# Memory rows of a recurrent attention block: transposed by VectorE out of PSUM ahead of the sum, with the output's sum moved behind the next q projection

## The chip, the cores and the metric

The kernel runs on one core of a Trainium2 chip. The metric is device time in microseconds (us); three runs of the kernel before gave 1015.4, 1016.96 and 1017.25, median 1016.96. The engines are named as in the profile: PE is TensorE (PEld its weight loads), DVE is VectorE, ACT is ScalarE, POOL is GpSimd, SP is the engine that issues most DMAs.

## What is computed

A transformer block over one sequence of 2048 rows of 640 numbers. The attention is recurrent: the sequence is cut into 64 segments of 32 rows, and each segment is attended together with 8 memory rows, which are the first 8 output rows of the segment before. So segment s+1 cannot be projected in full before the output projection of segment s has given its memory rows. A feed-forward network (640 to 1728 to 640, squared ReLU) follows.

```python
mem = mem0
for s in range(n_seg):                       # 64 segments of 32 rows
    xs = x[:, s * seg_len:(s + 1) * seg_len, :]      # x is layer-normed
    h = jnp.concatenate([mem, xs], axis=1)           # 8 + 32 rows
    q, k, v = (jnp.einsum('btd,dhe->bhte', h, W) for W in (Wq, Wk, Wv))   # 32 heads of 128
    p = _softmax(jnp.where(mask, jnp.einsum('bhqe,bhke->bhqk', q, k) * scale, -1e9))
    o = jnp.einsum('bhte,hed->btd', jnp.einsum('bhqk,bhke->bhqe', p, v), Wo)
    mem = o[:, :M, :]
    outs.append(o[:, M:, :])
h = x + jnp.concatenate(outs, axis=1)
h2 = h + ffn(_layernorm(h))
```

## The kernel before, in words

**Start.** SP issues the loads of wv, wq and wk (`load_w`, L117: five DMAs of 128 partitions and 1 MB each per weight, chunk c holding rows 128c to 128c+127 of the weight) and then wo in six DMAs (`load_wo`). `start` projects the first rows while these come in; step 0's output projection needs wo.

**A step** (`step`, L379) is one segment. The 8 memory rows and the first 24 rows of the segment are 32 "main" rows; the last 8 rows of each segment ("tails") are projected four segments at a time and ahead of need, in small units that serve as filling work. The main rows stand transposed in `hT4` (128 partitions x 5 chunks x 4 segments x 32 rows), so that a projection (`proj`, L196) is twenty matmuls with 32 columns of `hT4` as weights and 512 columns of wq, wk or wv streaming, five chunks for each of four column groups of PE. In order PE does: q half 0, k half 0, q half 1, k half 1 (L206), the memory rows' scores (`scores`, L417, which needs q spread by POOL into `qz` and k half 0 flipped), a part of v, the tokens' scores (L488), the rest of v between softmax parts, attention values (L448, L453), then the output projection `wo_rounds` (L238) into `pw`. Each projection is copied out of PSUM by ACT into `row` (L222, L224, L404 for the last one in halves) and flipped in 32x32 blocks by DVE into qT or kT (L227, L407).

**From output to memory rows.** `wo_rounds` puts four partial results into `pw`: partitions 64*kh + 32*ch + row, where kh is one of two halves of the heads that must be summed and ch one of two halves of the 640 columns. `wo_out` (L241) copies the upper 64 partitions by ACT (`otmp`, L245, 64x320 f32) and adds on DVE (`o`, L246). The columns in each half are interleaved by 64 (`wov2`, L229), so that `mem_to_hT` (L312) can turn the 8 memory rows with twenty small matmuls against an identity (`pm`, L316) and one DVE copy (L318) into the next segment's columns of `hT4`. `store_main` (L339) sends the other 24 rows to DRAM (`o_all`).

**Order.** Each engine runs its instructions in the order in which the program issues them; nothing reorders them. Filling work sits in lists: `fill` (tail projections L206 and the tails' output projection L238 on `oTt`), `late` (DVE flips and LayerNorm statistics, run at the start of the next step), `mid` and `win`. Ahead of `mem_to_hT` a step runs four or six fill units, and the rest behind it. `token_out` (ACT, two copies, L364) stands behind `wo_out`. `tk`, `otmp` and other short-lived tiles share one buffer; `sm`, `pm` and `pw` share one PSUM bank (pool `chn`).

**Afterwards** the FFN runs in four blocks of 512 rows; `prep_sum` (L631) adds the attention's rows to x.

Of the kernel before, what the change touches and what calls it, by code (L numbers as in the profile page):

```python
# [9 lines left out]
ALU = mybir.AluOpType  # L10
AX = mybir.AxisListType
F32 = mybir.dt.float32
BF16 = mybir.dt.bfloat16
# [3 lines left out]
def kernel(  # L17
# [16 lines left out]
    nc = tc.nc  # L34
    _, S, D = A_x.shape
    _, H, E = A_Wq.shape
    M = A_mem0.shape[1]
    SEG = 32
    G = 4
    HG = H // G  # L40
    HE = H * E
    EG = HE // G
    DC = D // 128
    DH = D // 2
    NB = S // 128
    NS = S // SEG
    HD = 24
# [13 lines left out]
    const = ctx.enter_context(tc.tile_pool(name="const", bufs=1))  # L61
    mm = ctx.enter_context(tc.tile_pool(name="mm", bufs=3, space=bass.MemoryType.PSUM))
    chn = ctx.enter_context(tc.tile_pool(name="chn", bufs=1, space=bass.MemoryType.PSUM))
# [4 lines left out]
    s1 = ctx.enter_context(tc.tile_pool(name="s1", bufs=1))  # L68
    s2 = ctx.enter_context(tc.tile_pool(name="s2", bufs=2))

    o_all = dram.tile([S, D], BF16)
# [4 lines left out]
    wo = wts.tile([128, H, D], BF16)  # L76

    ident = const.tile([128, 128], BF16)
    o_ring = [const.tile([128, DH], BF16, name="o%d" % k) for k in range(5)]
    o0 = o_ring[-1]  # L80
    nc.vector.memset(o0[0:64], 0.0)
    make_identity(nc, ident[:])
    mhalf = const.tile([128, 1], F32)
    nc.vector.memset(mhalf[:], -0.5)
# [11 lines left out]
    for g in range(G):  # L96
        r = slice(32 * g, 32 * g + 32)
# [6 lines left out]
    nc.vector.memset(oT[:], 0.0)  # L104
    oTts = [const.tile([128, H, 32], BF16, name="oTt%d" % k) for k in range(2)]

    for o in o_ring:
        nc.gpsimd.memset(o[64:128], 0.0)

    ctx.enter_context(tc.manual_schedule(engines=None))  # L110

    def head(p):
# [3 lines left out]

    def load_w(w, src):  # L117
        w2d = src.rearrange("d h e -> d (h e)")
        for c in range(DC):
            nc.sync.dma_start(out=w[:, c * HE:(c + 1) * HE], in_=w2d[c * 128:(c + 1) * 128, :])  # L120

    xts = {}

# [9 lines left out]
        xts["t", g] = xt  # L133

    load_x(0)
    for ch in range(2):
        nc.scalar.dma_start(out=o0[32 * ch:32 * ch + M, :].rearrange("m (c f) -> m c f", f=64),
                            in_=A_mem0[0].rearrange("m (c t f) -> t m c f", t=2, f=64)[ch])
    load_tail_rows(0)
    load_w(wv, A_Wv)  # L140

# [19 lines left out]
    hT4s, hTts, tails = {}, {}, {}  # L161
# [5 lines left out]
    def ln_norm(b):  # L167
        mv, rs = xns[b]
        xn = s1.tile([128, D], BF16, tag="xn", name="xn")
        xt = xts.pop(b)  # L170
        nc.vector.tensor_scalar(out=xn[:], in0=xt[:], scalar1=mv[:, 0:1], scalar2=rs[:, 0:1],
                                op0=ALU.subtract, op1=ALU.mult)
        xns[b] = xn

    def ln_transpose(b):
# [50 lines left out]
    def flip(row, dst, n):  # L226
        nc.vector.transpose(out=dst[:, n * 16:(n + 1) * 16, 0:32], in_=row.rearrange("p (h e) -> p h e", e=32))  # L227

    wov2 = wo[:].rearrange("p h (c t f) -> p h t c f", t=2, f=64)  # L229

    def wo_rounds(lhs, pw, h0, h1):

        for h in range(h0, h1):
            for kh in range(2):
                for ch in range(2):
                    j = kh * 2 + ch
                    p = h // 8 * 16 + kh * 8 + h % 8
                    nc.tensor.matmul(pw[32 * j:32 * j + 32, 0:DH], lhsT=lhs(p), rhs=wov2[:, head(p), ch],  # L238
                                     start=(h == 0), stop=(h == 15))

    def wo_out(pw):  # L241
        o = o_ring[0]
        o_ring.append(o_ring.pop(0))
        tmp = s1.tile([128, DH], F32, tag="tk", name="otmp")
        nc.scalar.copy(out=tmp[0:64], in_=pw[64:128, 0:DH])  # L245
        nc.vector.tensor_tensor(out=o[0:64], in0=pw[0:64, 0:DH], in1=tmp[0:64], op=ALU.add)  # L246
        return o

    fill, late, mid, win = [], [], [], []

    def run(q, n):
        while n > 0 and q:
            q.pop(0)()
            n -= 1
# [38 lines left out]
    def wo_tail_units(b):  # L293
        st = {}

        def out():
            o = wo_out(st["ps"])
            dst = o_all[:].rearrange("(b s t) d -> b s t d", s=4, t=SEG)
            for ch in range(2):
                nc.sync.dma_start(out=dst[b, :, HD:SEG, ch * DH:(ch + 1) * DH], in_=o[32 * ch:32 * ch + 32, :])  # L300

        def unit(k):
            def f():
                if k == 0:
                    st["ps"] = mmtile()
                wo_rounds(lambda p: oTts[b % 2][:, p, :], st["ps"], k * 16 // 10, (k + 1) * 16 // 10)
                if k == 9:
                    late.append(out)
            return f
        return [unit(k) for k in range(10)]  # L310

    def mem_to_hT(o, hT4, sp):  # L312
        pm = chn.tile([128, 512], F32, tag="ch", name="pm")
        for c in range(DC):
            for q in range(4):
                nc.tensor.matmul(pm[32 * q:32 * q + 32, c * M:(c + 1) * M], lhsT=o[:, (2 * c + q % 2) * 32:(2 * c + q % 2 + 1) * 32],  # L316
                                 rhs=ident[:, q // 2 * 32:q // 2 * 32 + M], start=True, stop=True)
        nc.vector.tensor_copy(out=hT4[:, :, sp, 0:M], in_=pm[:, 0:DC * M].rearrange("p (c m) -> p c m", m=M))  # L318

    def tails_in(b, sp, which="qk", h0=0, h1=H):  # L320
        q, k = [tails[b][w][:].rearrange("p h (k s) -> p h s k", s=4)[:, h0:h1, sp, :] if w in which else None for w in "qk"]
# [5 lines left out]
    vt4s, stores = {}, []  # L327
    vt_d = dram.tile([NB, 4, 128, 2 * E], BF16)

# [8 lines left out]

    def store_main(o, s):  # L339
        for ch in range(2):  # L340
            nc.sync.dma_start(out=o_all[s * SEG:s * SEG + HD, ch * DH:(ch + 1) * DH],
                              in_=o[32 * ch + M:32 * ch + 32, :])

    oTg = oT[:].rearrange("p (n g j) q -> p n g j q", n=2, g=G)
    back = []
# [33 lines left out]
    def step(b, sp, v=None):  # L379
        s = b * 4 + sp  # L380
        last = s == NS - 1
        hT4 = hT4s[b]
# [4 lines left out]
        run(late, 3)  # L387
        if sp == 1 and b + 1 < NB:
            tails_v_in(b + 1, nc.sync)

        def project(which, w, dst, n, between=None):
            if ready:
                if between:
                    between()
                return
            ps = mmtile()
            proj(w, "columns", lhs, n, ps, 0, DC)
            row = rowtile()
            if not between:
                evac_row(which, row[:], ps[:])  # L400
                flip(row[:], dst, n)
                return
            for u in range(2):
                nc.scalar.copy(out=row[:, u * 256:(u + 1) * 256], in_=ps[:, u * 256:(u + 1) * 256])  # L404
            between()
            for u in range(2):
                nc.vector.transpose(out=dst[:, n * 16 + u * 8:n * 16 + u * 8 + 8, 0:32],  # L407
                                    in_=row[:, u * 256:(u + 1) * 256].rearrange("p (h e) -> p h e", e=32))
# [49 lines left out]
            evac(n == 0, oTg[:, n, :, :, 0:M], po[:, :, c0:c0 + 4 * M].rearrange("p g (j m) -> p g j m", m=M))  # L458

        project("q", wq, qT, 0)  # L460
        if not last and not ready:
            spread(0)
        if not last:
# [55 lines left out]
        tk = s1.tile([128, HG, NK], F32, tag="tk", name="tk")  # L519
# [5 lines left out]
        pw = chn.tile([128, 512], F32, tag="ch", name="pw")  # L525
# [4 lines left out]
        if not last:  # L530
# [14 lines left out]
                                op=ALU.mult)  # L545
        pk = s1.tile([128, HG, 32], BF16, tag="pk", name="pk")
        nc.gpsimd.tensor_tensor(out=pk[:], in0=ek[:, :, 0:SEG], in1=rk[:].unsqueeze(2).to_broadcast([128, HG, SEG]),
                                op=ALU.mult)

        o = wo_out(pw)  # L550
        if s:
            token_out(s - 1, po)
        if s > 1:
            store_main(o, s - 2)
        outs = [win.pop(0)()] if win else []
        for f in outs:
            f()
        if not last:
            run(fill, 4 if outs else 6)
            mem_to_hT(o, hT4s[(s + 1) // 4], (s + 1) % 4)  # L560
            tails_in((s + 1) // 4, (s + 1) % 4)
        run(mid, 2)
        run(fill, 100)
# [3 lines left out]
        for u in range(2):  # L567
            nc.gpsimd.tensor_tensor(out=pTx[:, u], in0=pTt[:, u, HD:32].unsqueeze(1).to_broadcast([128, 4, TL]),
                                    in1=same[:], op=ALU.mult)
# [60 lines left out]

    def prep_sum(t, k, got):  # L631
        ot, fx = got
        fv = fx.rearrange("p (c t f) -> p t c f", t=2, f=64)
        nc.vector.tensor_tensor(out=fv, in0=ot.rearrange("p (t c f) -> p t c f", t=2, f=64), in1=fv, op=ALU.add)
        return fx

    def prep_norm(t, k, ht, mv, rs):
# [81 lines left out]
    load_w(wq, A_Wq)  # L719
    ln_stats(("t", 0))  # L720
    ln_transpose(0)()
    mem_to_hT(o0, hT4s[0], 0)
    ln_norm(("t", 0))
    load_w(wk, A_Wk)
    load_wo()
# [2 lines left out]
    v0 = start()  # L728
    halves = [h for b in range(8, NB) for h in (tail_units(b, "v")[:DC], tail_units(b, "v")[DC:])]
    for b in range(NB):  # L730
        for sp in range(4):
            run(soon, 1)
            if sp == 0 and b + 2 < NB:
                load_x(b + 2)
# [5 lines left out]
            if b == 0 and sp == 2:  # L740
                fill += tail_units(7, "v")[DC:]
            if 0 < b < NB - 1 and 0 < sp < 3:
                fill += tail_units(b + 1, "vqk"[sp])
# [28 lines left out]
            e = b * 4 + sp - (NS - 7)  # L772
# [30 lines left out]
    for t in range(S // NT):  # L803
# [6 lines left out]
        for fc in range(FC):  # L810
            ps = mmtile()
            for c in range(DC):
                if fc < FFULL:
                    nc.tensor.matmul(ps[:], lhsT=w1[:, c, fc * 128:(fc + 1) * 128], rhs=hnT[:, c, :],  # L814
                                     start=(c == 0), stop=(c == DC - 1))
                    continue
                for hh in range(2):
                    nc.tensor.matmul(ps[FREM * hh:FREM * (hh + 1), 0:HT], lhsT=w1[:, c, fc * 128:F],
                                     rhs=hnT[:, c, HT * hh:HT * (hh + 1)], start=(c == 0), stop=(c == DC - 1))
            w = NT if fc < FFULL else HT  # L820
            r = rs_[fc % 4]
            nc.scalar.activation(out=r[:, 0:w], in_=ps[:, 0:w], func=ACT.Relu, bias=b1f[:, fc:fc + 1], scale=1.0)  # L822
            nc.vector.tensor_tensor(out=f1T[:, fc, 0:w], in0=r[:, 0:w], in1=r[:, 0:w], op=ALU.mult)  # L823
            if more and fc >= 1 and (fc - 1) // 3 < NK4:
                k, stage = divmod(fc - 1, 3)
# [10 lines left out]
        for q in range(NK4):  # L836
# [6 lines left out]
            for hh in range(2):  # L843
                k = pr + 2 * hh
                for fc in range(FFULL):
                    nc.tensor.matmul(y[:, hh, 0:DH], lhsT=f1T[:, fc, k * 128:(k + 1) * 128], rhs=w2[:, fc, cs],  # L846
                                     start=(fc == 0), stop=False, skip_group_check=True)
                if more and q and (hh == 0 or q == 1):
                    k = q if hh == 0 and q > 1 else hh
                    prep_pe(t + 1, k, hn_[k])()  # L850
            for hh in range(2):
                r = slice(FREM * hh, FREM * (hh + 1))
                nc.tensor.matmul(y[:, hh, 0:DH], lhsT=f1T[r, FFULL, pr * 128:(pr + 1) * 128], rhs=w2[r, FFULL, cs],
                                 start=False, stop=True, skip_group_check=True)
            for hh in range(2):
                b = t * NK4 + pr + 2 * hh
# [38 lines left out]
```

## Time and profile before

| what | value |
|---|---|
| runs | 1015.4, 1016.96, 1017.25 us |
| the profiled execution, its span | 1017.01 us, 1014.9 us |
| busy share PE, PEld, DVE, ACT, POOL | 94%, 56%, 62%, 53%, 31% |
| chain that ended last, by engine | PE 74%, DVE 11%, DMA 7%, ACT 4% |
| L206 projections wq, wk, wv on hT | 160.0, 159.4, 165.2 us busy |
| L238 output projection pw | 181.9 us busy |
| L316 memory rows' matmuls, L318 their copy | 18.4 us (1280), 12.8 us (64 of 0.200) |
| L245 otmp, L246 o out of pw | 27.9 us (66 of 0.422), 31.8 us (66 of 0.482) |
| mean TensorE clock | 0.996 |

A line of the waits reads: engine and line that waited, what it waited for, total us, how often, longest us. A line of the timeline reads: start in us, duration, engine, line, operation, output and inputs, shapes, count of merged instructions, and in brackets the idle time of the engine before it and what ended it. A line of the chain reads: start, share of the path, what. Busy time of PE is time with at least one matmul in flight; matmuls overlap, so PE can be "busy" and still be late.

### The profile page before, as it was taken

How to read it: one execution, taken by the hardware profiler on the slowest of the kernel's cores; microseconds unless marked ns; L12 is line 12 of the kernel's file. 1: busy time of each engine (PE TensorE's matmuls, PEld its weight loads, DVE VectorE, ACT ScalarE, POOL GpSimd, SP SyncE). 2: the span in 40 equal slices, each digit the busy share in tenths (PEclk: the TensorE clock that was granted, in tenths of full speed). 3: DMA queues.
4: the chain of work that ended last, by engine and by line, in shares of the span. 5: the costliest groups of instructions: out<-in, count | busy, mean ns of one | idle time of the engine just before them, and what ended most of it. 6: DMA issues, size and time to landing. Idle time of an engine off the chain costs nothing.

```text
span 1014.9 us, 57673 instructions
## 1 busy us (share of the span) xinstructions
PE 957.6 (94%) x26191; PEld 564.2 (56%) x26200; DVE 629.8 (62%) x1868; ACT 536.2 (53%) x1229; POOL 311.5 (31%) x867
## 2 busy tenths in 40 slices
PE   5779899999999999999999999999999999899998
PEld 2345465555655565555555655566555555555565
DVE  2256676766676757676767676766666677466532
ACT  3336555555565655655655555655555555533431
POOL 1023333333333333333333333333232333433210
PEclk9989999999999999999999999999999999999999
DMA  9950101000101010000000000000000110612200
GB/s 363 397 193 21 23 7 31 7 25 6 32 11 29 7 34 15 20 17 25 17 20 17 24 18 14 22 20 22 13 22 8 48 34 7 221 40 66 78 27 26
DMA packets 39109, 51.51 MB, mean 51 GB/s; under 512 B 5968, under 2 KB 35024, under 8 KB 36944
## 3 DMA queue, kind: packets, MB, share of 16 engines
q1 hardware_dynamic: 38080, 47.48, 14.1%
q8 instruction: 205, 3.36, 1.4%
q10 hardware_dynamic: 784, 0.34, 0.1%
q14 instruction: 40, 0.33, 0.1%
HBM read 38.37 MB, written 9.44 MB: 47 GB/s over the span
## 4 chain that ended last, share of the span: by engine, by line
PE 74%; DVE 11%; DMA 7%; ACT 4%; issue 2%; SPq 1%; ACTq 0%; DVEq 0%; POOL 0%; POOLq 0%
PE ps L206 38%; PE pw L238 14%; PE y L846 5%; DVE kT L407 5%; PE ps L814 4%; PE ps L238 3%; PE po L448 2%; ACT row L404 2%; PE po L354 2%; DMA vt_d<-row 2%; DMA wq<-in_B_w_dram 2%; DVE pTm L439 2%; DVE pmem L434 1%; DMA wv<-in_A_Wv_dram 1%; DMA wo<-in_A_Wo_dram 1%
## 5 line engine op out<-in xcount | busy, mean ns | idle before, releaser
L206 PEld LDWEIGHTS <-hT 128*32 128x32 bf16 x7680 | 194.9, 96 | 176.9 <-issue 14.7
L238 PE MATMUL pw<-wo,oT 128*32 128x320 bf16 x4224 | 181.9, 300 | 7.9 <-issue 3.9
L206 PE MATMUL ps<-wv,hT 128*32 128x512 bf16 x2520 | 165.2, 379 | 0.7 <-ACT v L497 0.7
L206 PE MATMUL ps<-wq,hT 128*32 128x512 bf16 x2520 | 160.0, 382 | 5.3 <-DVE hT L318 5.3
L206 PE MATMUL ps<-wk,hT 128*32 128x512 bf16 x2520 | 159.4, 381 | 0.1
L238 PEld LDWEIGHTS <-oT 128*32 128x32 bf16 x4224 | 103.8, 96 | 59.9 <-ACT oT L215 13.4
L222 ACT ACTIVATE row<-ps 128x512 bf16<-128x512 f32 x156 | 93.3, 599 | 76.0 <-PE ps L206 74.3
L227 DVE STREAM_TRANSPOSE qT<-row 128x512 bf16<-128x512 bf16 x128 | 90.3, 705 | 66.6 <-ACT row L222 66.5
L523 POOL TENSOR_TENSOR tk<-tk,mxk 128x320 f32<-128x320 f32 x64 | 46.2, 723 | 239.9 <-DVE mxk L522 239.9
L540 DVE TENSOR_REDUCE zk<-ek 128x8 f32<-128x320 bf16 x64 | 31.1, 486 | 91.3 <-ACT ek L538 91.3
L373 POOL COPY qz<-qT 128x96 bf16<-128x96 bf16 x126 | 33.4, 265 | 175.2 <-DVE qT L227 105.5
L224 ACT CAST row<-ps 128x512 bf16<-128x512 f32 x115 | 68.0, 591 | 33.0 <-PE ps L206 32.9
L206 PEld LDWEIGHTS <-hTt 128*32 128x32 bf16 x1920 | 53.3, 96 | 31.5 <-issue 0.8
L364 ACT CAST oT<-po 128x512 bf16<-128x512 f32 x128 | 68.7, 589 | 1.6
L227 DVE STREAM_TRANSPOSE kT<-row 128x512 bf16<-128x512 bf16 x65 | 46.1, 709 | 31.2 <-ACT row L224 31.2
L846 PE MATMUL y<-wq,wk 128*128 128x320 bf16 x416 | 61.1, 299 | 0.4 <-DVE wk L823 0.2
L516 ACT CAST v<-ps 128x512 bf16<-128x512 f32 x63 | 36.9, 585 | 39.2 <-PE ps L206 39.2
L404 ACT CAST row<-ps 128x256 bf16<-128x256 f32 x126 | 40.8, 375 | 30.0 <-PE ps L206 30.0
L245 ACT COPY otmp<-pw 64x320 f32<-64x320 f32 x66 | 27.9, 422 | 52.8 <-PE pw L238 52.8
L246 DVE TENSOR_TENSOR o<-pw,otmp 64x320 bf16<-64x320 f32 x66 | 31.8, 482 | 33.1 <-ACT otmp L245 33.1
L822 ACT ACTIVATE wv<-ps,b1f 128x512 bf16<-128x512 f32 (+1 forms) x56 | 37.6, 672 | 27.3 <-PE ps L814 26.9
L417 PEld LDWEIGHTS <-qz 128*32 128x32 bf16 x2016 | 34.3, 95 | 31.2 <-POOL qz L373 2.0
(111 smaller groups left out, 1609.7 us busy)
## 6 DMA issues: line engine op xcount, KB each, us to landing
wv<-in_A_Wv_dram SPq DMA_DIRECT2D x5, 1024.0 KB
wq<-in_A_Wq_dram SPq DMA_DIRECT2D x5, 1024.0 KB
wk<-in_A_Wk_dram SPq DMA_DIRECT2D x5, 1024.0 KB
vt<-vt_d SPq DMA_DIRECT2D x60, 64.0 KB
xt<-in_A_x_dram SPq DMA_DIRECT2D x20, 160.0 KB
vt_d<-row SPq DMA_DIRECT2D x22, 128.0 KB
wo<-in_A_Wo_dram SPq DMA_DIRECT2D x2, 1280.0 KB
wo<-in_A_Wo_dram SPq DMA_DIRECT2D x4, 640.0 KB
```

The costliest lines, as they stand in the source:

```text
L206: nc.tensor.matmul(ps[32 * k:32 * k + 32, :], lhsT=lhs(c), rhs=wr[:, c, n, k], start=(c == 0), stop=(c == DC - 1))
L222: nc.scalar.mul(out=row, in_=ps, mul=scale)
L224: nc.scalar.copy(out=row, in_=ps)
L227: nc.vector.transpose(out=dst[:, n * 16:(n + 1) * 16, 0:32], in_=row.rearrange("p (h e) -> p h e", e=32))
L238: nc.tensor.matmul(pw[32 * j:32 * j + 32, 0:DH], lhsT=lhs(p), rhs=wov2[:, head(p), ch], start=(h == 0), stop=(h == 15))
L364: nc.scalar.copy(out=oTg[:, n, :, :, M:NK], in_=po[:, :, n * 128:(n + 1) * 128].rearrange("p g (j q) -> p g j q", q=32))
L404: nc.scalar.copy(out=row[:, u * 256:(u + 1) * 256], in_=ps[:, u * 256:(u + 1) * 256])
L407: nc.vector.transpose(out=dst[:, n * 16 + u * 8:n * 16 + u * 8 + 8, 0:32], in_=row[:, u * 256:(u + 1) * 256].rearrange("p (h e) -> p h e", ...
L523: nc.gpsimd.tensor_tensor(out=tk[:], in0=tk[:], in1=mxk[:].unsqueeze(2).to_broadcast([128, HG, NK]), op=ALU.subtract)
L814: nc.tensor.matmul(ps[:], lhsT=w1[:, c, fc * 128:(fc + 1) * 128], rhs=hnT[:, c, :], start=(c == 0), stop=(c == DC - 1))
L822: nc.scalar.activation(out=r[:, 0:w], in_=ps[:, 0:w], func=ACT.Relu, bias=b1f[:, fc:fc + 1], scale=1.0)
L846: nc.tensor.matmul(y[:, hh, 0:DH], lhsT=f1T[:, fc, k * 128:(k + 1) * 128], rhs=w2[:, fc, cs], start=(fc == 0), stop=False, skip_group_chec ...
```

## The change

The memory rows no longer go through PE. Two DVE block transposes take all of `pw` out of PSUM in f32, 160 columns each; ACT copies the eight memory columns of the upper 64 partitions down (L255 of the changed kernel), and DVE adds both head halves into `hT4` in two adds of 64x40. Block transposes leave column 160q + 32c + f of the model dimension on partition 32q + f of chunk c. So the model dimension is permuted throughout: the weights' rows are loaded in 32-partition pieces (four DMAs per chunk in place of one), the LayerNorm writes its columns in that order, `wov2`, `store_main`, the tails' store and `prep_sum` follow, and mem0 is loaded as four pieces and turned by DVE.

The sum of the whole output (`wo_out`) and its store are put off: they run in the next step, right behind q half 0 (`owed`), on ACT and DVE. In the last step they stay where they were. All fill units now run behind the output projection with nothing between them; `token_out` stands behind the memory rows' transposes and copies.

```diff
-    o_ring = [const.tile([128, DH], BF16, name="o%d" % k) for k in range(5)]
+    o_ring = [const.tile([64, DH], BF16, name="o%d" % k) for k in range(5)]
+    o0 = const.tile([128, DC, 32], BF16, name="om")
...
     def load_w(w, src):
         w2d = src.rearrange("d h e -> d (h e)")
+        rows = w2d.rearrange("(q c f) e -> c q f e", q=4, c=DC)
         for c in range(DC):
-            nc.sync.dma_start(out=w[:, c * HE:(c + 1) * HE], in_=w2d[c * 128:(c + 1) * 128, :])
+            for q in range(4):
+                nc.sync.dma_start(out=w[32 * q:32 * q + 32, c * HE:(c + 1) * HE], in_=rows[c][q])
...
-        nc.vector.tensor_scalar(out=xn[:], in0=xt[:], scalar1=mv[:, 0:1], scalar2=rs[:, 0:1],
-                                op0=ALU.subtract, op1=ALU.mult)
+        nc.vector.tensor_scalar(out=xn[:].rearrange("p (c q f) -> p c q f", c=DC, q=4),
+                                in0=xt[:].rearrange("p (q c f) -> p c q f", c=DC, q=4),
+                                scalar1=mv[:, 0:1], scalar2=rs[:, 0:1], op0=ALU.subtract, op1=ALU.mult)
...
-    wov2 = wo[:].rearrange("p h (c t f) -> p h t c f", t=2, f=64)
+    wov2 = wo[:].rearrange("p h (a t f) -> p h t a f", a=2, t=2)
...
+    def mem_to_hT(pw, hT4, sp):
+        tr = s1.tile([128, 2, DC, 32], F32, tag="tk", name="otr")
+        tc_ = s1.tile([64, 2, DC, M], F32, tag="otc", name="otc")
+        for a in range(2):
+            nc.vector.transpose(out=tr[:, a], in_=pw[:, a * DQ:(a + 1) * DQ].rearrange("p (c f) -> p c f", f=32))
+            nc.scalar.copy(out=tc_[:, a], in_=tr[64:128, a, :, 0:M])
+        for a in range(2):
+            nc.vector.tensor_tensor(out=hT4[64 * a:64 * a + 64, :, sp, 0:M], in0=tr[0:64, a, :, 0:M], in1=tc_[:, a], op=ALU.add)
...
-    def mem_to_hT(o, hT4, sp):
-        pm = chn.tile([128, 512], F32, tag="ch", name="pm")
-        for c in range(DC):
-            for q in range(4):
-                nc.tensor.matmul(pm[32 * q:32 * q + 32, c * M:(c + 1) * M], lhsT=o[:, (2 * c + q % 2) * 32:(2 * c + q % 2 + 1) * 32],
-                                 rhs=ident[:, q // 2 * 32:q // 2 * 32 + M], start=True, stop=True)
-        nc.vector.tensor_copy(out=hT4[:, :, sp, 0:M], in_=pm[:, 0:DC * M].rearrange("p (c m) -> p c m", m=M))
+    def mem0_to_hT(hT4):
+        mt = s1.tile([128, DC, 32], BF16, tag="pk", name="mt")
+        nc.vector.transpose(out=mt[:], in_=o0[:])
+        nc.vector.tensor_copy(out=hT4[:, :, 0, 0:M], in_=mt[:, :, 0:M])
...
         project("q", wq, qT, 0)
+        run(owed, 1)
...
-        o = wo_out(pw)
+        if not last:
+            mem_to_hT(pw, hT4s[(s + 1) // 4], (s + 1) % 4)
         if s:
             token_out(s - 1, po)
-        if s > 1:
-            store_main(o, s - 2)
+
+        def rows_out():
+            o = wo_out(pw)
+            if s > 1:
+                store_main(o, s - 2)
         outs = [win.pop(0)()] if win else []
         for f in outs:
             f()
-        if not last:
-            run(fill, 4 if outs else 6)
-            mem_to_hT(o, hT4s[(s + 1) // 4], (s + 1) % 4)
+        if last:
+            rows_out()
+        else:
+            owed.append(rows_out)
             tails_in((s + 1) // 4, (s + 1) % 4)
```

## The prediction

> **What bounds the kernel now.** I read the page first: TensorE (PE) is busy for 94% of the span, so what counts is PE's instructions and the places where PE stands still. The list of waits shows the two that belong to the memory rows, in both of PE's rows (PE for matmuls, PEld for weight loads):
>
> ```profile
> PEld L316 <- DVE o L246: 20.8, 47, 1.4
> ...
> PEld L206 <- DVE hT L318: 13.2, 49, 0.5
> ...
> PE pm L316 <- DVE o L246: 6.4, 10, 1.1
> ...
> PE ps L206 <- DVE hT L318: 5.3, 15, 0.4
> ```
>
> In most of the 63 steps that have a next one PE waits twice: for the sum o (L246) and for the turned rows hT (L318). Idle PEld time counts only where no matmul covers it, so I went to the timeline of a typical step:
>
> ```profile
> 502.50 0.42 ACT L245 COPY otmp<-pw 64x320 f32<-64x320 f32 x1 [0.54 <-PE pw L238]
> 502.51 0.20 DVE L542 RECIPROCAL rk<-zk 128x8 f32<-128x8 f32 x1
> ...
> 502.95 0.48 DVE L246 TENSOR_TENSOR o<-pw,otmp 64x320 bf16<-64x320 f32 x1 [0.23 <-ACT otmp L245]
> ...
> 503.51 0.28 PE L316 MATMUL pm<-ident,o 128*32 128x8 bf16 x20
> ...
> 504.28 1.25 PE L206 MATMUL ps<-wq,hT 128*32 128x512 bf16 x20
> ...
> 504.54 1.30 DVE L227 STREAM_TRANSPOSE kTt<-row 128x512 bf16<-128x512 bf16 x2
> ```
>
> The last matmul of pw starts at 502.09 (the pw row ahead of these starts at 501.12 and lasts 1.27, and one matmul takes 0.30). The first q matmul on the new rows starts at 504.28, 2.19 us later. Between them lie 24 + 12 matmuls of filling work on either side of L316's twenty; twenty projection matmuls start every 1.08 us, 0.054 each, so they need 1.94, and 0.21 is lost. The chain of waits then tells what sets the end later in the step:
>
> ```profile
> 503.79 5.01 PE ps L206 x70
> 508.82 0.38 ACT row L404
> 509.23 0.77 DVE kT L407 x2
> 510.00 0.06 DVE rm L432
> ...
> 510.50 0.26 DVE pTm L439
> ```
>
> It leaves PE at 508.8, goes through ScalarE's half copy and VectorE until 510.76 and returns to PE. An earlier q therefore shortens the step only if VectorE (DVE) is free at about 509.0. The fourth view is the busy time by windows; its last two columns are the DMA engines' busy share and GB/s:
>
> ```profile
> 118.40:122.20 3.80, 3.80 (x108) 1.95 (x100) 2.73 (x6) 2.34 (x7) 1.50 (x6) 1.00 0.23 71
> 3.40:44.40 41.00, 27.68 (x459) 13.54 (x460) 8.22 (x26) 14.77 (x24) 3.71 (x12) 1.00 1.02 408
> ```
>
> While wv, wq and wk come in (the second row), all DMA engines are full; wo follows, the chain goes through its landing, and step 0's pw starts right behind it at 60.13. The first 60 us are a DMA queue, the rest is PE.
>
> **Step by step: the memory rows.** Removed from each step: twenty L316 matmuls (0.13 of PE's order: the wk work resumes 0.13 after pm starts), the copy L318 (0.20), and from the path to q the sum, 0.42 + 0.48. Added: two VectorE transposes 128x160 f32, two ScalarE copies and two adds of 64x40. No row shows the transpose from f32. Bounds: 128x64 bf16 took 0.245 and 128x256 took 0.401; an f32 copy out of PSUM took 0.292 for 128 columns and 0.200 for 40, so 160 at that slope give 0.33. If a 4-byte element counts as two, it is 320 bf16 columns, 0.47. I take 0.33, the row with the same source and type. Neighbours on VectorE that don't depend on each other overlap by 0.07 (two kTt flips take 1.30, one 0.69).
>
> In the step above: VectorE's reciprocal ends at 502.71, 0.2 behind the point where pw is readable (502.50), and stands ahead in its queue. Transposes 502.75 to 503.08 and 503.01 to 503.34; the second copy 503.39 to 503.59 (0.20, as L318's 40 columns); the second add 503.63 to 503.80; 0.18 later, as now, q could start: 503.98. PE's filling work ends at 504.07, so q starts there: **0.21 earlier**. By the same count the 34 steps with 34 to 36 projection matmuls of fill gain 0.21 each (7.1); 14 steps with 60 wo matmuls gain the 0.14 of the removed PE work (2.0); 7 steps with 16 and 6 with none, where the chain and no fill decides (L316 waits 1.43 at 167.81), go from 2.03 to about 1.92 (1.4); two with 28 gain 0.3 each (0.6). Together 11.1.
>
> **What is queued behind.** ScalarE now waits for the transposes before it copies, and token_out (L364, 1.07) stands behind: it starts at 503.61, not 502.94. The two fill copies follow until 505.76 (now 505.09), q's copy at 505.68 (now 505.59). The moved sum adds 0.42 there before k's copy, at 506.55 still ahead of now (506.67). On VectorE the two kTt flips run 505.2 to 506.5, q's flip 506.44 to 507.15, the moved add 507.08 to 507.56, k's flip 507.49 to 508.20 (now 508.00), the second q flip 508.17 to 508.88. scores(0) wants k's flip at about 508.39; it fits with 0.15 to spare, and VectorE is free for 509.0 less 0.21. So the moved sum is covered, but by little, in the 28 steps that carry two flips; I take **-9** instead of -11.1. The later store of the sum waits on SP some 4 us longer; behind it stand loads that are used a step or more later.
>
> Costed at nothing: the LayerNorm's permuted write (0.59, off the chain), the FFN's simpler sum, mem0's transpose (it waits for wv anyway, whose last matmuls come at 17.4), and smaller stores (30 KB a step, DMA share near 0.1 in mid-run). Without cover each would be under 0.5 us once.
>
> **The weights.** The permutation splits each 1 MB load into four of 32 partitions: 60 DMAs in place of 15, for 15.73 MB. SP takes about 0.43 to issue one of the first, 26 us for sixty, below the 38.6 us that 15.73 MB need at 408 GB/s: issue is hidden. Unknown is the rate of a DMA that writes 32 partitions. One end is the rate of now (0). The only loads into 32 partitions in the trace, vt (L337, the first window), moved 71 GB/s at share 0.23: as they stand, 15.73 MB would take 222 us, +183, the other end, which I think far, because those kept only 0.23 of the engines busy. Per busy engine vt gives 71/0.23 = 309 GB/s, or 50.9 us, +12. If writes into a quarter of the partitions keep half of the write side busy, 204 GB/s, 77.1 us, +38. I take the middle of the last two, 256 GB/s: 61.4 us, **+23**. Nothing hides it: wo is queued behind, and step 0's pw waits for wo.
>
> The Trainium skill, SBUF — State Buffer, section Door 1: The DMA port swizzle, says that partitions 0 to 31 reach 8 of the 16 ports that DMAs write through, as 0 to 63 do, and gives 189 GB/s for 32 and 328 for 128 partitions at 1 MiB; its section on issuing two DMAs to hit both halves says that these serialize. By that rule alone the loads would go at about half rate and the sum would be that of the half-rate rival below. No run here shows it; vt's 309 per busy share speaks for a milder effect, and engines that drift apart would write different halves at once.
>
> **Sum.** The profiled execution took 1017.0 (span 1014.9 plus 2.1 around it), the median of the runs is 1016.96, so nothing is to be corrected. 1017.0 + 23 - 9 = **1031**.
>
> **Rivals.**
> - *Loads at half rate* (204 GB/s): +38 - 9, **1046**. For it: four neighbouring DMAs of a chunk go out in the same order on every engine. Against: the engines need not stay in step. Chance 0.13; my forecast's own case, +12 to +33, has 0.45.
> - *The loads keep their rate* (other side): the queue stays full, the rate is that of the DMA engines (share 1.02) and not of the partitions, and the gain in the steps is left: **1008**, faster. Place: before 60 us. It decides at an added load time of 9 us, a rate of 330 GB/s: above it the change gains. Chance 0.30.
> - *VectorE's queue eats the gain, loads free*: with transposes of 0.47 the second add ends at 504.08 and q starts at 504.26, no gain; the second q flip ends 0.06 later than now, and 28 steps lose up to 0.1: **1020**. Chance 0.07.
> - *Gain and loads cancel* (added load time of about 9): **1017**, 0.05.
>
> **How the numbers follow.** Slower 0.45 + 0.13 + 0.07 = 0.65, faster 0.30, same 0.05, with 0.2% (2 us) as about what a measurement of this kernel can tell from no change. The range for 8 in 10 runs from 1007, which leaves out about a third of the faster case, to 1046, half of the half-rate case. The +183 end is left out. The slower cases alone run from 1019 to 1046.
>
> **What would show it.** Step 0's first pw: at 60 with loads at rate, at 83 by my forecast, at 98 at half rate; the GB/s in the window of the three loads says which. In a mid-run step: q 2.0 us behind the last pw (now 2.19), transposes of 0.33 (0.47 for the third rival), VectorE's half flip of k at 7.0 behind the last pw (now 7.14). If PE waits for the scores, the moved sum was not covered. The forecast is wrong if the loads keep over 330 GB/s, or if the steps get longer.

## The result, and the profile after

The changed kernel takes 1053.01 us (median of 4 runs, 1051.68 to 1059.69); the kernel before, run beside it, 1017.11 (4 runs, 1015.4 to 1018.2). The ratio is **1.0368 [1.0322, 1.0414]**: slower. The forecast was 1031 with a range of 1007 to 1046, so the sign is right and the time lies outside the range.

The two profiled executions (1051.68 with a span of 1049.7; 1017.01 with 1014.9) differ by 34.8 us of span. I divide both at two places that can be found in each, the last `pw` matmul of step 0 and that of step 62 (steps count from 0, and step 62 is the last one that hands on memory rows):

| part | before | after | difference |
|---|---|---|---|
| up to the last `pw` matmul of step 0 | 60.55 | 98.28 | +37.7 |
| from there to that of step 62 | 802.26 | 796.1 | -6.2 |
| from there to the end (the last step and the FFN) | 152.06 | 155.3 | +3.3 |

**The first part** shows in the page's 40 slices (26 us each) of the changed kernel: the granted clock in tenths, the DMA engines' busy share in tenths, and GB/s.

```profile
PEclk9877999999999999999999999999999999999999
DMA  9999010100010001000100000000000110512200
GB/s 210 206 206 288 29 24 8 29 8 23 12 29 12 23 13 34 13 23 12 29 12 23 13 28 13 23 13 27 14 24 8 47 33 6 187 54 76 76 26 26
```

Three slices, 79 us, run at 206 to 210 GB/s with full DMA engines. The busy time by windows puts a number to it: first the loads of wv, wq and wk, then the loads behind them. The columns are the stretch, its length, the busy time and count of instructions of PE, PEld, DVE, ACT and POOL, the granted clock, the DMA engines' busy share and GB/s.

```profile
3.40:80.50 77.10, 39.65 (x439) 15.21 (x440) 8.89 (x27) 14.23 (x24) 3.71 (x12) 0.87 0.97 213
...
80.50:98.00 17.50, 13.10 (x279) 6.54 (x282) 8.38 (x23) 6.48 (x15) 2.89 (x7) 0.79 1.01 333
```

The DMA engines are nearly as busy as in the kernel before (0.97 against 1.02) and move half as much (213 GB/s against 408). In the timeline of SP (start, duration, queue, line, tile) one can see the loads push back on the engine that issues them:

```profile
1.91 17.00 SPq L120 DMA_DIRECT2D wv<-in_A_Wv_dram  x20
...
20.95 25.39 SPq L120 DMA_DIRECT2D wq<-in_A_Wq_dram  x20
...
47.31 24.93 SPq L120 DMA_DIRECT2D wk<-in_A_Wk_dram  x20
...
73.08 15.31 SPq L145 DMA_DIRECT2D wo<-in_A_Wo_dram  x6
```

Issuing wq's twenty DMAs takes 25.39 us. They carry 5.2 MB, which is 206 GB/s: SP issues no faster than the queue empties. wo, next in the program, is only issued from 73.08 on (from 37.24 before). PE stands still meanwhile, by the waits (what waited, for what: us, times, longest); in the kernel before, these three come to 2.7, 1.6 and 1.6:

```profile
PE pa L206 <- DMA wk<-in_A_Wk_dram: 11.5, 4, 3.9
PE pa L206 <- DMA wv<-in_A_Wv_dram: 11.2, 4, 3.0
PE pa L206 <- DMA wq<-in_A_Wq_dram: 11.1, 4, 3.6
```

**The second part**, one step of the changed kernel (timeline; the last `pw` matmul starts at 523.24):

```profile
523.37 2.12 PE L206 MATMUL ps<-wq,hTt 128*32 128x512 bf16 x36
523.66 0.20 DVE L553 RECIPROCAL rk<-zk 128x8 f32<-128x8 f32 x1
523.78 0.54 DVE L254 STREAM_TRANSPOSE otr<-pw 128x160 f32<-128x160 f32 x2
...
524.12 0.45 ACT L255 COPY otc<-otr 64x40 f32<-64x40 f32 x2 [1.02 <-DVE otr L254]
524.26 0.61 POOL L558 TENSOR_TENSOR pk<-ek,rk 128x256 bf16<-128x256 bf16 x1
524.38 0.78 DVE L257 TENSOR_TENSOR hT<-otr,otc 64x40 bf16<-64x40 f32 x2
...
525.31 1.25 PE L206 MATMUL ps<-wq,hT 128*32 128x512 bf16 x20
...
527.30 0.42 ACT L245 COPY otmp<-pw 64x320 f32<-64x320 f32 x1
...
527.97 0.44 DVE L246 TENSOR_TENSOR o<-pw,otmp 64x320 bf16<-64x320 f32 x1
...
530.26 0.77 DVE L417 STREAM_TRANSPOSE kT<-row 128x256 bf16<-128x256 bf16 x2
```

The fill's 36 matmuls start 0.13 behind the last `pw` matmul and need 1.94, and q follows them without a gap, 2.07 behind `pw` (2.19 before). The turned rows are ready at 525.16, ahead of that. The sum, now behind q's copy, ends at 528.41, and VectorE is free for k's half at 530.26, 7.02 behind `pw` (7.14 before). Over all 63 steps the time from the last `pw` matmul to q falls by 9.5 us; some 3.4 of it is lost again, scattered over the rest of the steps; single profiles of unchanged steps differ by more than that (see the change without the split).

**The third part** is taken up at the end of the next section.

### The profile page after: what moved, and what is told of

Its sections match the earlier page's. It is cut to its first block, busy times and chain, and to the rows that moved or that the text cites. A ratio compares the mean times of both kernels' runs of the same rounds, so it can differ in the third digit from the quotient of the medians.

```text
span 1049.7 us, 55684 instructions
## 1 busy us (share of the span) xinstructions
PE 964.2 (92%) x24911; PEld 565.1 (54%) x24920; DVE 682.5 (65%) x2058; ACT 559.1 (53%) x1355; POOL 306.9 (29%) x862
## 4 chain that ended last, share of the span: by engine, by line
PE 67%; DVE 16%; DMA 7%; ACT 5%; issue 3%; SPq 1%; POOL 1%; ACTq 0%; DVEq 0%; POOLq 0%
PE ps L206 36%; PE pw L238 12%; PE y L861 5%; PE ps L829 5%; DVE kT L417 4%; PE ps L238 3%; DMA wv<-in_A_Wv_dram 2%; PE po L458 2%; ACT row L414 2%; DVE pTm L449 2%; DVE pmem L444 2%; DMA wq<-in_A_Wq_dram 2%; PE po L364 1%; DMA wo<-in_A_Wo_dram 1%; DVE pmem L445 1%
## 5 line engine op out<-in xcount | busy, mean ns | idle before, releaser
L206 PEld LDWEIGHTS <-hT 128*32 128x32 bf16 x7680 | 197.1, 96 | 216.6 <-issue 39.7
L206 PEld LDWEIGHTS <-hTt 128*32 128x32 bf16 x1920 | 58.7, 103 | 46.7 <-issue 13.7
L255 ACT COPY otc<-otr 64x40 f32<-64x40 f32 x126 | 28.1, 223 | 76.7 <-DVE otr L254 76.2
L224 ACT CAST row<-ps 128x512 bf16<-128x512 f32 x115 | 65.2, 585 | 5.4 <-PE ps L206 3.6
L417 DVE STREAM_TRANSPOSE kT<-row 128x256 bf16<-128x256 bf16 x126 | 48.5, 423 | 2.6 <-ACT row L414 0.2
```

The costliest lines, as they stand in the source:

```text
L206: nc.tensor.matmul(ps[32 * k:32 * k + 32, :], lhsT=lhs(c), rhs=wr[:, c, n, k], start=(c == 0), stop=(c == DC - 1))
L224: nc.scalar.copy(out=row, in_=ps)
```

## The experiments

**Theories of the weights.** After this profile, 38 us of loads had to be explained. (a) A piece of 32 partitions is written at half rate, whatever else is in flight. (b) Sixty small DMAs in place of fifteen large ones cost it, whichever partitions they write. (c) Neighbouring pieces go to the same quarter of the partitions at the same time, so that another order or a second queue would bring the rate back.

*e1_split32* is the kernel before with nothing but the split, in natural order:

```diff
         for c in range(DC):
-            nc.sync.dma_start(out=w[:, c * HE:(c + 1) * HE], in_=w2d[c * 128:(c + 1) * 128, :])
+            for q in range(4):
+                r = slice(32 * q, 32 * q + 32)
+                nc.sync.dma_start(out=w[r, c * HE:(c + 1) * HE], in_=w2d[c * 128 + 32 * q:c * 128 + 32 * q + 32, :])
```

> The kernel before, with each 1 MB weight load issued as four DMAs of 32 partitions in natural row order; nothing else is changed. Theory P (a DMA into 32 partitions is written at half the stream's rate): 15.73 MB at about 211 GB/s as in the changed kernel, first output projection near 98 us instead of 60, total 1017 + 37 = 1054. Theory R (it is the permuted order of the weights' rows that is slow to read): no change, 1017. Theory S (sixty DMAs of 256 KB cost more than fifteen of 1 MB): as P here, told apart by the split along columns.

Measured: 1056.13 us, ratio 1.0383 [1.0363, 1.0402]; step 0's last `pw` matmul at 99.2. The split alone costs all that the first part lost. Its windows:

```profile
3.40:80.00 76.60, 40.16 (x459) 15.06 (x459) 8.05 (x26) 14.76 (x24) 3.73 (x12) 0.84 0.96 210
```

*e2_splitcols* has the same sixty DMAs of 256 KB, but each over all 128 partitions and a quarter of the columns:

```diff
+            for q in range(4):
+                f = slice(q * EG, (q + 1) * EG)
+                nc.sync.dma_start(out=w[:, c * HE + q * EG:c * HE + (q + 1) * EG], in_=w2d[c * 128:(c + 1) * 128, f])
```

> The kernel before, with each 1 MB weight load issued as four DMAs of 128 partitions and a quarter of the columns: sixty DMAs of 256 KB again. Theory P: the rate stays near 400 GB/s, 1017 to 1019. Theory S: half rate as in the changed kernel, 1050 or more.

Measured: 1029.64 us, 1.0113 [1.0089, 1.0136]. Its windows:

```profile
3.40:44.40 41.00, 26.37 (x367) 11.30 (x371) 7.61 (x26) 13.16 (x22) 2.71 (x7) 1.00 0.96 319
```

Rows of 2 KB in place of 8 cost a fifth of the rate and 12 us, so (b) isn't free in this form, and the run met neither of the two forecasts; but 319 is far from 210, with rows four times shorter than those of the split. Sixty DMAs of 256 KB are not what halves the rate; what is left is that each writes a quarter of the partitions. (A piece of 32 rows is also read from a smaller stretch of DRAM. No run spreads such a read over all partitions, so the two sides of the transfer are not told apart.)

*e5_split64*: two DMAs of 64 partitions per chunk (as e1, with `range(2)` and 64).

> The kernel before, with each 1 MB weight load issued as two DMAs of 64 partitions in natural row order. Theory H (the halves 0 to 63 and 64 to 127 are two sides, and a DMA in one half gets half the rate, whether it fills it or not): 210 to 215 GB/s again, as with 32 partitions, 1055. Rival (the rate goes with the number of partitions, and 32 happened to give half): more than 300 GB/s, 1030 or less.

Measured: 1054.7 us in one run (before beside it: 1015.93), step 0's `pw` at 99.9. Twice the partitions, and no faster:

```profile
3.40:80.00 76.60, 38.18 (x455) 13.96 (x459) 8.03 (x26) 14.69 (x24) 3.81 (x12) 0.89 0.95 208
```

*e4_twoqueues*: the changed kernel, with the upper two quarters of wv issued on ACT's queue.

```diff
+                eng = nc.scalar if w is wv and q > 1 else nc.sync
-                nc.sync.dma_start(out=w[32 * q:32 * q + 32, c * HE:(c + 1) * HE], in_=rows[c][q])
+                eng.dma_start(out=w[32 * q:32 * q + 32, c * HE:(c + 1) * HE], in_=rows[c][q])
```

> The changed kernel with wv's two upper quarters (partitions 64 to 127) issued on ACT's queue and the two lower ones on SP's; wq and wk stay on SP's queue. Theory P with the engines in step (each half of the partitions idles in turn because one queue serves them in order): each DMA engine alternates between the halves, wv comes in at over 300 GB/s in the window from 3 to 20 us, some 10 us less in all. Rival: a load into 32 partitions is slow by itself, whatever goes on beside it: 210 to 225 GB/s in that window, no change from the 1053 of the changed kernel.

Measured: 1043.81 us in one run. The windows of this kernel while both queues hold weights, and after that:

```profile
4.00:28.00 24.00, 7.48 (x70) 3.21 (x74) 4.16 (x17) 3.34 (x4) 1.58 (x4) 1.00 1.02 230
28.00:77.00 49.00, 27.00 (x377) 11.31 (x369) 4.19 (x8) 11.25 (x20) 2.09 (x8) 0.85 0.97 217
```

In that first window both queues carry weights (2.90 and 2.62 MB), and 230 is no more than lies between the changed kernel's 240 (3 to 12 us) and 221 (12 to 20 us); in the same two windows e4 has 249 and 225. Pieces of both halves in flight at once don't bring the rate back. The time did fall by 9 us, as theory P had it, but not in the way that it says: of the 7.7 us between the two profiles' spans 4.4 lie ahead of step 0's `pw` (93.9 against 98.28), some 6% of the time that the loads take, and 2.7 in the third part, which the loads don't touch.

*e10_split32_alt* is e1 with the pieces in the order 0, 2, 1, 3; *e11_split16_alt* has pieces of 16 partitions in the order 0, 4, 1, 5, 2, 6, 3, 7, so that each pair in the queue lies 64 partitions apart.

```diff
-            for q in range(4):
+            for q in (0, 2, 1, 3):
```

> The split of the weight loads into 32 partitions, natural order, with the four pieces of a chunk issued as 0, 2, 1, 3, so that neighbours in the queue lie in opposite halves of the partitions. Theory K (all engines work on the same piece at a time, and a piece has the rate of its half): 210 GB/s again, 1056. Rival D (engines drift by a piece or more, and alternating more finely lets both halves be written at once): 250 to 400 GB/s, 1020 to 1045.

> The same with pieces of 16 partitions (one row of 8 KB for each engine), issued alternately from the lower and the upper half: 120 loads of 128 KB. Theory K: half rate or less, since 16 neighbouring partitions are a quarter of one half's reach: 105 to 210 GB/s, 1056 to 1130. Rival D: a drift of a single row is enough to write both halves at once, 300 GB/s or more, 1035 or less.

Measured, one run each, before beside them at 1017.71: 1049.45 us for e10 and 1095.75 for e11. The windows of e10:

```profile
3.40:73.00 69.60, 36.50 (x443) 14.61 (x443) 8.12 (x26) 14.61 (x24) 3.72 (x12) 0.92 0.95 222
```

and of e11:

```profile
3.40:100.00 96.60, 38.11 (x391) 14.39 (x391) 8.14 (x26) 14.14 (x23) 3.71 (x12) 0.81 0.92 136
```

Both lie nearer to theory K than to rival D. The order is worth 5%, and smaller pieces are worse. (a) stands: in this queue a piece of 32 or 64 partitions runs at half rate, nearly whatever stands beside it. How the DMA engines share out the pieces, and so why the order is worth anything, stays open; e11 doesn't tell its fewer partitions from its smaller DMAs (128 KB).

**The change without the split.** If the model dimension stays in its natural order, the weights need no split. *e3_natural* gets there by picking wo's columns in blocks of 32 by turns, so that the block transposes drop the memory rows on the natural partitions; `load_w`, the LayerNorm and the stores are as before. All else of the change stays.

```diff
-    wov2 = wo[:].rearrange("p h (a t f) -> p h t a f", a=2, t=2)
+    wov2 = wo[:].rearrange("p h (a t f) -> p h t a f", t=2, f=32)
...
-            nc.vector.transpose(out=tr[:, a], in_=pw[:, a * DQ:(a + 1) * DQ].rearrange("p (c f) -> p c f", f=32))
+            nc.vector.transpose(out=tr[:, a], in_=pw[:, 0:DH].rearrange("p (c a f) -> p a c f", a=2, f=32)[:, a])
```

> The changed kernel with the permutation moved from the weights' rows to the columns of the output projection, so that each weight is loaded by five DMAs of 128 partitions as before, and the LayerNorm and the stores are as before; transposes, copies, adds and the moved sum are as changed. Theory P: loads at rate again, first output projection near 60 us; the steps keep their gain of about 6 and the FFN its 3: 1011 to 1014. If the step's part was really a loss that hid in the shift: 1018 or more.

Measured: **1010.37 us, 0.9929 [0.9911, 0.9946]**, 7 us faster than the kernel before and 43 faster than the changed one. Step 0's last `pw` matmul starts at 60.45 (60.55 before), the loads run as before:

```profile
3.40:44.40 41.00, 27.32 (x439) 13.22 (x440) 8.35 (x27) 14.77 (x24) 3.70 (x12) 1.00 1.01 409
```

The steps (the second part) take 792.9, 9.4 less than before, and the time from `pw` to q alone is 9.35 less. That these two agree is partly luck. In the steady steps q comes 0.12 earlier and the step is 0.09 shorter; the rest of the sum comes from uneven steps, and these differ from profile to profile: e1, e2, e5, e10 and e11, whose steps are those of the kernel before, take 796.1 to 802.1 in this part, and e4, with the changed steps, 795.4. The medians of the times (1010.37 against 1017.44) are the better measure of the gain, about 7 us.

**The moved sum.** In *e7_natural_nodefer*, e3's sum of the whole output stays in its own step.

```diff
-        if last:
-            rows_out()
-        else:
-            owed.append(rows_out)
+        rows_out()
+        if not last:
             tails_in((s + 1) // 4, (s + 1) % 4)
```

> The natural-order version with the whole output's sum left in its own step, behind token_out, instead of behind the next q projection. Theory M (the moved sum is worth time, because in place it stands on ScalarE and VectorE ahead of the fill's copies and flips and so delays the next q's copy): up to 0.3 in each of the 34 steps with copies, 1012 to 1020. Rival (both engines have room there, moving it is worth nothing): 1009 to 1012.

Measured: 1029.61 us, 1.0135 [1.0114, 1.0155]; the steps take 811.4, 18.5 more than in e3, while the time from `pw` to q grows by 0.07 in all 63 together. The loss, twice what theory M allowed, is behind q. The same step in the timelines, first e3 (last `pw` matmul at 533.885):

```profile
536.09 1.07 ACT L219 ACTIVATE row<-ps 128x512 bf16<-128x512 f32 x2
...
536.71 1.30 DVE L224 STREAM_TRANSPOSE qTt<-row 128x512 bf16<-128x512 bf16 x2
...
537.94 0.42 ACT L242 COPY otmp<-pw 64x320 f32<-64x320 f32 x1
...
540.90 0.77 DVE L411 STREAM_TRANSPOSE kT<-row 128x256 bf16<-128x256 bf16 x2
```

and e7 (last `pw` matmul at 545.086):

```profile
547.41 0.42 ACT L242 COPY otmp<-pw 64x320 f32<-64x320 f32 x1
...
547.86 1.57 ACT L219 ACTIVATE row<-ps 128x512 bf16<-128x512 f32 x3
...
547.86 0.48 DVE L243 TENSOR_TENSOR o<-pw,otmp 64x320 bf16<-64x320 f32 x1 [0.86 <-ACT otmp L242]
...
549.25 1.25 DVE L224 STREAM_TRANSPOSE qTt<-row 128x512 bf16<-128x512 bf16 x2
...
552.38 0.77 DVE L411 STREAM_TRANSPOSE kT<-row 128x256 bf16<-128x256 bf16 x2
```

With the sum in its own step, `otmp` stands on ScalarE ahead of the fill's two copies and q's: the first of them starts 2.77 behind `pw` where e3 has 2.20. VectorE waits 0.86 for `otmp` and then spends 0.48 on the sum, so its first flip starts 4.16 behind `pw` where e3 has 2.83. Most of that is made up again, but k's half flip still comes 7.29 behind `pw` where e3 has it at 7.02. Such steps are 0.27 to 0.5 longer, and 23 of them make up some 8 of the 18.5 us. 4.7 more lie in one early step of e7, in which PE waits 2.92 us for the scores and the clock is halved for 3.4 us, and the rest was not followed. So with the sum in this place, ahead of the fill's copies, turning the rows on VectorE is slower than the kernel before even with the loads at full rate. The sum in its own step but behind the fill was not run.

**The adds.** One row of the changed kernel had no place in the prediction: the adds (L257), by the durations of a line (min/median/max in ns).

```profile
L257 DVE TENSOR_TENSOR hT<-otr,otc x126: 191/195/549, 99.9 to 896.2; 64x40 bf16<-64x40 f32 x126
```

In the step above the first add runs 0.55 and the second 0.19, while POOL's `pk` runs beside the first. One theory was that an add of two SBUF operands waits for a POOL instruction that reads SBUF, and that this delays q; the rival, that the fill covers it. *e6_natural_psum* lets ScalarE copy into free columns of `pw`'s PSUM tile, so that the add has one operand there; *e8_psum_onecopy* does so with one copy after both transposes; *e9_sbuf_onecopy* is e8's control, one copy into SBUF.

```diff
-        tc_ = s1.tile([64, 2, DC, M], F32, tag="otc", name="otc")
+        tc_ = pw[0:64, DH:DH + 2 * DC * M].rearrange("p (a c m) -> p a c m", a=2, m=M)
...
-            nc.scalar.copy(out=tc_[:, a], in_=tr[64:128, a, :, 0:M])
+        nc.scalar.copy(out=tc_, in_=tr[64:128, :, :, 0:M])
```

(the first pair of lines is e6, both are e8, the second alone is e9, with `otc` as its output)

> The natural-order version with the two small ScalarE copies written to free columns of pw's PSUM bank instead of SBUF, so that the adds read one operand from PSUM. Theory L (the adds of 64x40, 0.320 on average, wait for POOL's pk and pkt, which read SBUF at the same time): adds of about 0.2, q starts 1.98 behind the last pw in place of 2.07 in the steps with 36 fill matmuls and up to 0.4 earlier in the steps with little fill: 34 x 0.09 + 10 x 0.3 = 6 less, 1004 to 1007. Rival (the adds are slow by their short strided rows): adds stay at 0.3, 1010.

> The natural-order version with both transposes first, then one ScalarE copy of 64x80 into free columns of pw's PSUM bank, then the two adds: the adds read PSUM as in the version with two copies there, but no transpose stands between two writes to that tile. Theory L (what is left of the wait for the rows is the first add's wait for POOL): adds of 0.19 without the 0.55, q starts at the end of the fill, 1.98 behind the last pw in place of 2.07 in the steps with 36 fill matmuls, 34 x 0.09 + some 15 x 0.1 = 4 to 5 less than the natural-order version, 1005 to 1007. Rival (the PSUM bank costs by itself, whatever the order): 1015 or more, as in the version with two copies.

> The natural-order version with both transposes first, then one ScalarE copy of 64x80 to SBUF, then the two adds: the control of the run beside it. Theory L: the first add starts later, still under POOL's pk and still 0.4 to 0.55 long, q no earlier than in the natural-order version: 1009 to 1012. Rival (the gain of the version beside it, if there is one, comes from the single copy): the same time as that version.

Measured: e6 1024.04 us, 1.0077 [1.0061, 1.0094]; e8 1012.73, 0.9962 [0.995, 0.9974]; e9 1011.06, 0.9939 [0.9926, 0.9951]. The adds of e8, and then of e9:

```profile
L254 DVE TENSOR_TENSOR hT<-otr,pw x126: 186/189/192, 62.0 to 856.4; 64x40 bf16<-64x40 f32 x126
```

```profile
L254 DVE TENSOR_TENSOR hT<-otr,otc x126: 191/195/286, 61.9 to 860.6; 64x40 bf16<-64x40 f32 x126
```

In the changed kernel 46 of the 63 first adds take over 0.25, and each of them ends 0.05 behind POOL's `pk`. In e8 44 first adds start while `pk` runs, and none takes more than 192 ns. So the operand in PSUM ends the stretch. In e9 it is not gone, as its theory had it, but the single copy lets the add start later, and 0.29 is left of the 0.55. But q still starts 2.07 behind `pw` in the filled steps of e8, e9 and e3 alike, and e8 gains no time: the stretch is real and is covered by the fill. e6, 14 us slower than e3, doesn't tell on this; none of its adds starts while `pk` runs. It put a new wait where the old one was, as its waits show: the second transpose reads `pw` and now stands behind ScalarE's write into the same tile.

```profile
DVE otr L251 <- ACT pw L252: 19.8, 63, 0.6
...
DVE hT L254 <- ACT pw L252: 16.0, 63, 0.3
```

**The last 3.3 us.** The third part takes 155.3 in the changed kernel, but also 154.7 in e3, which loads its weights at full rate, and 152.7 in e4, which loads them at about half. A stretch of 3.4 us at half the granted clock near 927 us lies in it, and e1, where no step was changed, and e3, whose loads keep their rate, have such a stretch too (at 910 to 920 and 870 to 890). In the windows of the changed kernel and of e1 it shows in the clock's column:

```profile
920.00:930.00 10.00, 7.37 (x81) 3.60 (x82) 6.04 (x17) 2.75 (x5) 5.67 (x6) 0.85 0.42 123
...
910.00:920.00 10.00, 7.07 (x198) 4.21 (x191) 1.65 (x5) 2.95 (x7) 2.38 (x6) 0.83 1.02 343
```

Over the thirteen profiles the part goes with this stretch: the nine that have one take 153.7 to 155.3, the four that have none (the kernel before, e4, e5 and e10) 152.1 to 152.8. So it follows neither the loads nor the steps. What brings the stretch about, and how much of the 3.3 us is the clock's own cost, is open.

## Why the prediction was wrong, point by point

- **The weights: this is the step that failed.** Forecast +23, measured +37.7 up to step 0's `pw`. The path was right (the loads, then wo, then `pw`), and so was the lower bound of the rate; the term was mis-sized, because I took the middle of 309 and 204 GB/s, and it was 213. The half-rate rival (+38, `pw` at 98) had it nearly to the microsecond, with a chance of 0.13. The upper end, 309, came from dividing vt's 71 GB/s by its busy share of 0.23. That quotient supposes that more busy engines would each go as fast. In the loads the engines are busy at 0.97 and move 213, or 220 per share, where the kernel before is busy at 1.02 and moves 408: the share counts the time that packets take and doesn't show that they take twice as long. That engines which write into the same half slow each other fits this, but no trace shows it directly. The other argument, that engines drift apart and then write different halves, fell with e4 (230) and e10 (222).
- The rule that I weighed against it, in the Trainium skill, SBUF — State Buffer, section Door 1: The DMA port swizzle, has 32 and 64 partitions reach the same half of the ports. The traces agree in the sharpest place, 64 no faster than 32 (208 and 210). In size they lie above the section's 189 and 328 GB/s for 32 and 128 partitions, which are for single loads of 1 MiB (these runs: 210 and 408), and nearer to its limits for long ones, 218 and 436. The Trainium skill's section on issuing two DMAs to hit both halves, on the same page, says that they serialize; e4's 230 agrees.
- **"SP takes about 0.43 to issue", so issue is hidden.** Hidden it was, but SP was held 17 to 25 us per weight by the full queue, and the loads behind, wo first, were issued that much later. They were late in any case.
- **The loads keep their rate (1008).** Refuted by 213 GB/s, below the 330 from which it would have paid. As a price for the change without the split it is 2 us off: e3 gives 1010.37.
- **The steps: -9.** The changed kernel has -6.2, e3 -9.4 (by the medians of the times, -7). From `pw` to q the forecast's -9 (counted 11.1) is measured -9.5, with the parts otherwise, so the sum came out near by luck: the 38 steps at about 2.19 gain 0.15 on average, those with 36 matmuls of fill 0.12, and not 0.21. I read 0.21 as time in which PE waits for the rows. But the fill itself starts 0.13 behind the last `pw` matmul, its 36 matmuls need 1.94 and `pm`'s twenty 0.13, together 2.20, which is the 2.19 of the step that I worked from: PE lost nothing there but `pm`'s own 0.13. The 13 steps at 2.8 to 2.9 gain 0.14 (0.14 forecast), and the ten at 2.03 with little or no fill 0.18 (0.11 forecast). Why the changed kernel loses 3.4 us of it again and e3 none, I did not settle; 1.3 of it lies between the `pw` of steps 0 and 1, where the changed kernel has 6.8 us at half the granted clock and e3 none, and the rest is within what unchanged steps differ by.
- **Transposes 0.33**: 0.309 at the median, which fits a cost by the element, not by the byte (0.47), and the third rival falls. **Copies 0.20**: 0.22. **Adds**: 0.195 (0.17 taken), but up to 0.55 beside POOL, not foreseen and covered.
- **The moved sum, "covered, but by little"**: k's half flip at 7.02 (7.0 forecast). That it is covered was right; what it costs in its own step behind the turned rows (18.5 us in e7), in part by the copies and flips queued behind it, was not in the prediction, which counted only its absence from the way to q.
- **The range.** Its upper end was the middle of the half-rate case, so half of that case was outside by choice. With 0.13 for the case that the only row of such loads (71 GB/s) leaned to, the range was too narrow.

## What to carry to other kernels

A permutation that an on-chip transpose leaves behind is best absorbed where it costs no transfer: here in the order of wo's columns (1010.37 us) and not in the weights' rows (1053.01). A long load in pieces of 32 or 64 partitions is priced at the measured half rate, and a rate "per busy share" from a window with few busy engines is no bound for a full queue. Of an operation that is moved, ask what stood behind it in its engine's queue, and not only what waited for its result.

## What the runs showed of the hardware

- A weight load in pieces of 64 partitions is as slow as one of 32 (208 and 210 GB/s against 408 for 128), pieces of 16 partitions and 128 KB by turns of the halves give 136, and rows of 2 KB over all partitions 319, all with the DMA engines busy at 0.92 to 1.02.
- A VectorE add of two f32 operands in SBUF, 64x40, takes 0.195 us and up to 0.55 when POOL's `pk`, which reads SBUF, is running as it starts; with one operand in PSUM 0.192 at most beside the same instruction (e8). The Trainium skill, SBUF — State Buffer, section SBUF: two separate sides, tells of a port pair that VectorE, with two SBUF inputs, and a GpSimd instruction that reads SBUF hold by turns; these rows agree.
